# A state-space convolution with a gated token update: the second exponential table as raw products, sums finished in PSUM, and a written-out instruction order

## The chip, the core and the metric

The kernel runs on one core of one Trainium2 chip. A core has five instruction streams: PE (TensorE, matrix products into the accumulator memory PSUM), ACT (ScalarE, functions and scaled copies), DVE (VectorE, elementwise work), POOL (GpSimd) and SP (used here to issue transfers). They meet only at semaphores. The metric is device time in microseconds (us), the median of some runs.

## What is computed

A sequence of 2048 tokens with 512 channels goes through two branches and a sigmoid gate mixes them. Everything is bf16 in and out.

```python
g = sigmoid((x * gate_w).sum(-1, keepdims=True))     # x = A_u, [1, 2048, 512]
# branch a: long convolution by a diagonal state-space model, 128 states per channel
dt = exp(log_dt)[:, None];  A = A_re + 1j*A_im;  dB = dt*(B_re + 1j*B_im)
l = arange(2048).astype(bfloat16)                    # so large lags coincide
P = exp((dt*A)[:, :, None] * l[None, None, :])
K = einsum("dn,dnl,dn->dl", C, P, dB).real           # C = C_re + 1j*C_im
a = irfft(rfft(pad(x.T)) * rfft(pad(K)))[:, :2048].T + x * Dskip
# branch b: the 2 tokens with the largest x @ w_r get a feed-forward update
y = (silu(x_sel @ w_gate) * (x_sel @ w_up)) @ w_down * sigmoid(r_sel)
b = x + scatter_add(zeros, idx, y)
out = g * a + (1 - g) * b
```

## The kernel before

Channels are worked on in two halves of 256 (index h), tokens in two blocks of 1024 (blk). Transforms are matrix products with cosine and sine matrices; pm is the half of the frequencies, par the parity of a token, part the real or imaginary part. The stages, by the names in the code:

- **Parameters.** Six transposing transfers (`prm_t`) bring the 512 x 128 parameter matrices in with states on partitions. DVE makes the decay rate `AL`, the angle `B16` as a fraction of a turn, and the weights `WW`, C times dB.
- **Tables.** A lag is split as T1[s] + T2[j]: 32 coarse and 21 fine values. `exps1` and `exps2` take exponentials of both (ACT); `trig` scales the angles, takes sines, adds a quarter turn and takes sines again (ACT and DVE in turn); `tab1(h)` multiplies magnitude and sine into the first table TP, real and imaginary. `tab2(h)` makes 9 entries of the second table, multiplies them by `WW` (`cmul`, 9 entries wide) and gets the other 12 by two more complex products (8 and 4 wide): 26 DVE multiplies and adds per half. The magnitudes of half 1 are parked in DRAM and loaded back (`PK`).
- **Kernel values.** `kgen(h)` multiplies TP by the second table on PE, 64 groups of 4 channels, a real and an imaginary product of 84 columns (21 lags x 4 channels) each. Small products with rows of the identity (L765 to L771) keep the lags of the matching channel and bring lags to partitions: tile KC.
- **Spectra.** `kspec(h)` multiplies KC by seven operands KP of cosines and sines (`KUSE`), giving the kernel's spectrum KK for both blocks. `forward` gives the input's spectrum X: per block, group of frequencies, pm and part, eight products of 512 columns. For pm = 1 the odd tokens use a negated matrix NG, loaded again for each group. In block 1 one more product adds block 0's spectrum to it (L733, the carry).
- **Products.** `products(h, qd, blks)` multiplies spectra on DVE in pieces of 2048 and 1024 elements and leaves the result in X.
- **Router.** `routing` transposes the input on PE, gets the gate g and the router's scores, finds the two tokens, gathers them by products with one-hot columns and runs the feed-forward part. `xupd` adds the update to the input on PE (32 products of 512 columns) and ACT scales it by 1 - g, in place in U.
- **Output.** `inverse(h)` transforms X back in PSUM. ACT scales by g into YA and DVE adds it to U, or, for the last block of half 1, one DVE operation per 256 columns does both (L396). Sixteen transfers write the result.

The order of the work is not written by hand. Every operation is entered with what it reads and writes (`Prog.op`), a cost in us and a priority; `Prog.schedule` builds each engine's list by a simulation with these costs, choosing the operation that can start first, and where two engines can do an operation (`EV`, `SCL`, which copy or scale on ACT or DVE) the engine too. `Prog.emit` turns dependences into semaphore waits. The exponentials come first, then one load of ACT's function table, then the sines. Nearly all vector multiplies come from the helper `TT` (L389), copies out of PSUM from `EV` (L404), angle scalings from `SCL` (L408).

Of the kernel before, what the change touches and what calls it, by code (L numbers as in the profile page):

```python
# [58 lines left out]
class Prog:  # L59
# [119 lines left out]

    def emit(self, handles_sem, dsem):  # L180
# [53 lines left out]
    def run(self, e, h):  # L234
        last = None
        for o, waits in self.prog[e]:
            for k, v in waits:
                h.wait_ge(self.sems[k] if not isinstance(k, tuple) else self.dsem[k[1]], v)
            if o.tset is not None and o.tset % 2 != last:
                last = o.tset % 2  # L240
                if last:
                    h.preload_act_table_set("silu_and_others")
            r = o.fn(h)
            s, i = (self.dsem[o.sem], 16) if o.dma else (self.sems[e], 1)
            if isinstance(r, (list, tuple)):
                for x in r:
                    x.then_inc(s, i)
            else:
                r.then_inc(s, i)
        if e == SP:  # L250
            for o in self.finals:
                h.wait_ge(self.dsem[o.sem], 16 * o.n)
# [6 lines left out]
T2 = [0, 1, 2, 3, 258, 256, 512, 768, 4, 5, 6, 7, 262, 260, 516, 772, 1024, 1280, 1536, 1792, 2048]  # L259
T2BASE = [(0, 4), (13, 17), (8,)]  # L260
NJ = len(T2)
ANG2 = [124 + t for t in T2[:8]] + [1148, 1024, 4]
MAG2 = [None] + T2[1:8] + [1024, 4]
NM = len(MAG2)
KUSE = [(0, 0), (0, 1), (0, 2), (0, 3), (0, 4), (1, 4), (1, 5)]
# [13 lines left out]
def fwd_mats():  # L279
    th = theta(512)  # L280
    out = np.zeros((128, 2, 4, 2, 512))
    for par in range(2):
        for st in range(4):
            t = 256 * st + 2 * np.arange(128) + par
            out[:, par, st, 0] = np.cos(np.outer(t, th))
            out[:, par, st, 1] = -np.sin(np.outer(t, th))
    return out.reshape(128, -1)
# [12 lines left out]

def kspec_mats():
    lq = bf16_lag(np.arange(L))
# [6 lines left out]
    out = np.zeros((len(KUSE), 128, 2 * BLK))  # L309
    cover = np.zeros(L, dtype=bool)  # L310
    for q in sorted(set(lq.tolist())):
        j, s = where[q]
        for u, (i, jg) in enumerate(KUSE):
            if jg != j // 4:
                continue
            ls = np.nonzero(lq == q)[0]
            ls = ls[(ls >= BLK * i) & (ls < BLK * (i + 1))]
            cover[ls] = True
            t = ls - BLK * i
            out[u, 32 * (j % 4) + s, :BLK] = np.cos(np.outer(t, th)).sum(0)  # L320
            out[u, 32 * (j % 4) + s, BLK:] = (sg * np.sin(np.outer(t, th))).sum(0)
# [3 lines left out]

KB = 1024


def bass_gated_mix__ssm_conv_s4__moe_arch_mod__prompt_kernel(nc, A_u, A_A_re, A_A_im, A_B_re, A_B_im, A_C_re, A_C_im, A_log_dt, A_Dskip,
# [3 lines left out]
    eye = np.eye(128, dtype=np.float32)  # L333
    sgn = np.diag(np.where(np.arange(128) % 2 == 0, 1.0, -1.0))
    cb = np.concatenate([eye, np.zeros((128, 384), np.float32), sgn, -sgn], 1)
    cb_c = const(cb, "c_bf")
    cf = np.zeros((128, 160), np.float32)
    cf[:, 0:128] = eye
# [7 lines left out]
    cf[:, 147] = math.pi / 2  # L346
    cf_c = nc.inline_tensor(cf, "c_f32").ap()
    fm = fwd_mats()
    f_c = const(fm, "c_fwd")
    fn_c = const(-fm[:, 4096:], "c_fwdn")  # L350
# [3 lines left out]
    with ExitStack() as es:  # L354
# [8 lines left out]
        def B(name, off, nbytes, dt=BF):  # L363
            assert off + nbytes <= SBW and off % 2 == 0, (name, off, nbytes)
            return Buf(P, name, AR, "sb", int(off), int(nbytes), dt)
        class PB:
# [11 lines left out]
        def npe(n):  # L378
            return max(0.065, n * 0.00045)
# [33 lines left out]
        o_ = [190 * KB]  # L413
# [4 lines left out]
        CB = small("cb", 1536, BF); CF = small("cf", 640, F32); AL = small("al", 2048, F32); B16 = small("b16", 2048, F32)  # L418
        WW = small("ww", 2048, BF); SG = small("sg", 256, F32); SGB = small("sgb", 128, BF); RTS = small("rts", 1088, F32)
        OHT = small("oht", 64, BF); ZB = small("zb", 2048, BF); WL = small("wl", 16, BF); XS = small("xs", 16, BF)  # L420
        HB = small("hb", 448, BF); MSB = small("msb", 16, BF); DSK = small("dsk", 1024, BF); OHR = small("ohr", 4096, BF)
        assert o_[0] <= SBW, o_[0]
        oA, oB, oC, oD, oE, oF, oG, oI = [x * KB for x in (0, 16, 48, 64, 96, 117, 149, 170)]
        U = B("u", oA, 16 * KB)
        X = B("x", oB, 32 * KB)
        P.bufs.remove(X)
        XB = [[B("x%d%d" % (h_, k_), oB + (16 * h_ + 8 * k_) * KB, 8 * KB) for k_ in range(2)] for h_ in range(2)]
        xk = lambda h_, k_, *key: (XB[h_][k_], key)
        F = B("f", oC, 16 * KB)
        PRM = B("prm", oB, 6 * KB)  # L430
        LDT = B("ldt", oB + 6 * KB, 1 * KB); DTB = B("dtb", oB + 7 * KB, 1 * KB)
        TMP = [B("tmp%d" % i, oB + (8 + 2 * i) * KB, 2 * KB, F32) for i in range(4)]
        CM1 = B("cm1", oB + 16 * KB, 4 * KB, F32); CM2 = B("cm2", oB + 20 * KB, 4 * KB, F32); CMW = B("cmw", oB + 24 * KB, 4 * KB, F32)
        TP = [(B("tpi0", oD, 16 * KB), B("tpr0", oD + 16 * KB, 16 * KB)), (B("tpi1", oF, 16 * KB), B("tpr1", oF + 16 * KB, 16 * KB))]
        HQ = NJ * HC * 2
        TQ = [(B("tqi%d" % i, o, HQ), B("tqr%d" % i, o + HQ, HQ)) for i, o in enumerate((oE, oG))]
        XT = B("xt", oD, 16 * KB)
        WG = B("wg", oF, 14 * KB); WD = B("wd", oF, 14 * KB)
        WU = [B("wu%d" % i, oB + (8 + 16 * i) * KB, 7 * KB) for i in range(2)]
        EB = [B("eb%d" % i, o, NM * 512) for i, o in enumerate((oG, oE))]  # L440
        ST = B("st", oE, NM * 512)
        PK = Buf(P, "park", AR[:, :], "dram", 0, 4, BF)
        park = nc.dram_tensor("park", (128, NM * 256), BF).ap()
        QA = [B("qa%d" % i, o + NM * 512, 9 * KB) for i, o in enumerate((oG, oE))]
        BN = [(B("bni%d" % i, o + 14 * KB, KB), B("bnr%d" % i, o + 15 * KB, KB)) for i, o in enumerate((oG, oE))]
        NG = [B("ng%d" % i, oG + 16 * KB + 2 * i * KB, 2 * KB) for i in range(2)]
# [3 lines left out]
        KA = [B("ka0", oG, 64 * 84 * 2), B("ka1", oE, 64 * 84 * 2)]  # L450
        KC = [B("kc0", oD + 28 * KB, 3 * KB), B("kc1", oE + 11 * KB, 3 * KB)]
        KP = B("kp", oD, 28 * KB)
        KK = [B("kk0", oC, 16 * KB), B("kk1", oF, 16 * KB)]
        G = B("g", oF + 16 * KB, 16 * KB)
        PA = B("pa", oI, 4 * KB); PBb = B("pb", oI + 4 * KB, 4 * KB); PC = B("pc", oI + 8 * KB, 4 * KB); YY = B("yy", oI + 12 * KB, 4 * KB); YA = B("ya", oI + 16 * KB, 4 * KB)
# [4 lines left out]
        kgp = [PB("kg%d" % i, 2, i) for i in range(2)]  # L460
        mc = [0]
# [9 lines left out]
        def ngsrc(ft):  # L471
            return bass.AP(fn_c.tensor, fn_c.offset + ft * 128, [[4096, 128], [512, 8], [1, 128]])
# [9 lines left out]
        def prm_t(i):  # L482
            dp[0] -= 1e3
            P.op(SP, lambda h: h.dma_start_transpose(PRM(0, 128, i * D, (1, D)), dr(prm[i], 0, (128, D), (1, 128))), [], [(PRM, i)], cost=1.25, nbytes=131072, prio=dp[0])  # L484
        DQ([(LDT(0, 128, 0, (1, D)), dr(A_log_dt, 0, (0, 128), (1, D)))], [], [LDT], 131072, eng=ACT)
        DQ([(CB(0, 128, 0, (1, 768)), cb_c[:, :])], [], [CB], 196608, eng=ACT)
        P.op(ACT, ld_w, [], [WL], cost=1.0, n=2, nbytes=20000, dma=True, prio=2.5e5)
        prm_t(0)
        prm_t(1)
        for j in range(2):  # L490
            DQ([(U(0, 128, j * 8 * D, (2 * D, 4), (1, 2 * D)), dr(A_u, 1024 * j * D, (2 * D, 128), (256 * D, 4), (1, 2 * D)))], [], [(U, t) for t in range(8 * j, 8 * j + 8)], 1048576)
        for i in range(2, 6):
            prm_t(i)
        DQ([(F(0, 128, 0, (1, 8192)), f_c[:, :])], [], [F], 2097152)
        DQ([(CF(0, 128, 0, (1, 160)), cf_c[:, :])], [], [CF], 81920)
        for ft in range(2):
            DQ([(NG[ft](0, 128, 0, (128, 8), (1, 128)), ngsrc(ft))], [], [NG[ft]], 262144)
        DQ([(WG(0, 128, 0, (NF, 4), (1, NF)), dr(B_w_gate, 0, (NF, 128), (128 * NF, 4), (1, NF)))], [], [WG], 1835008)
        for buf, n in ((DSK, D), (OHR, L), (ZB, 2 * D)):
            P.op(POOL, lambda h, buf=buf, n=n: h.memset(buf(0, 128, 0, (1, n)), 0.0), [], [buf], cost=0.2 + n * 0.5e-3)  # L500
        DQ([(DSK(0, 1, 0, (1, D)), dr(A_Dskip, 0, (D, 1), (1, D)))], [], [DSK], 1024)

        IDN = lambda *a: CB(0, 128, *a)


        f512 = lambda b, c=0: b(0, 128, c, (1, D))
        AC(f512(DTB), f512(LDT), ACTF.Exp, [LDT], [DTB], tset=0)
        TT(f512(AL), f512(DTB), f512(PRM, 0), ALU.mult, [DTB, (PRM, 0)], [AL])
        TT(f512(TMP[0]), f512(DTB), f512(PRM, D), ALU.mult, [DTB, (PRM, 1)], [TMP[0]])
# [6 lines left out]
        def cbc(c):  # L516
            return PRM(0, 128, c, (0, 2), (1, D))
        TT(c2(CM1), c2(PRM, 2 * D), cbc(4 * D), ALU.mult, [(PRM, 2), (PRM, 3), (PRM, 4)], [CM1])
        TT(c2(CM2), c2(PRM, 2 * D), cbc(5 * D), ALU.mult, [(PRM, 2), (PRM, 3), (PRM, 5)], [CM2])
# [4 lines left out]
        for i in range(2):  # L524
            DQ([(WU[i](0, 128, 0, (NF, 2), (1, NF)), dr(B_w_up, 256 * NF * i, (NF, 128), (128 * NF, 2), (1, NF)))], [], [WU[i]], 917504)


# [9 lines left out]
        def exps2(ts):  # L537
            for b in (EB[0], ST):
# [415 lines left out]
```

## Time and profile before

The median of 3 runs is 193.42 us (193.13 to 194.49). The profiled execution has a span of 191.7 us.

| stretch of the span, us | PE busy | DVE busy | ACT busy | what runs |
|---|---|---|---|---|
| 0 to 40 | 24.93 | 24.23 | 33.39 | parameters, exponentials, router |
| 184 to 191.7 | 3.42 | 3.80 | 0.00 | last inverse, output |

The rows for the stretches in between, and the kernel's busiest groups, are read in the prediction. Of the groups not read there, these matter (group: line, engine, what, count, mean of one):

| group | count | mean ns |
|---|---|---|
| L731 PE, forward, 512 columns | 256 | 387 |
| L841 PE, inverse, 256 columns | 256 | 281 |
| L787 PE, spectra, 256 columns | 224 | 273 |
| L751 PE, table product, 84 columns | 256 | 200 |
| L404 ACT, copy of 1024 from f32 PSUM | 27 | 1021 |
| L404 DVE, the same | 5 | 1215 |
| L400 ACT, exponential of 512 | 41 | 619 |
| L400 ACT, sine of 1024 | 24 | 1052 |
| L408 ACT, angle scaling of 256 | 36 | 409 |
| L408 DVE, the same | 18 | 287 |
| L393 DVE, quarter turn added to 1024 | 12 | 681 |
| ACT, table load | 2 | 1283 |

A matmul's record is longer than the step from one to the next, since they are pipelined: the chain of waits shows the step. In the profile's lines, AR is the one SBUF buffer in which all tiles lie, and ps the PSUM.

### The profile page before, as it was taken

What the parts mean: (1) busy time and instruction counts of PE and PEld (TensorE: products, weight loads), DVE (VectorE), ACT (ScalarE), POOL (GpSimd) and SP (SyncE); (2) the same over time, 40 slices, a digit from 0 to 9 for tenths busy, and PEclk for the clock granted to TensorE, in tenths of its full rate; (3) what the DMA queues carried; (4) which work ended last, traced back from release to release, by engine and by line L of the source; (5) the groups of instructions that cost most, each with busy time, mean ns of one, the idle gap of its engine ahead of it and who ended that gap; (6) DMA issues with size and microseconds to landing.
All of it is one profiled execution on the core that took longest, in us unless ns stands there. A gap on an engine that the chain in (4) does not pass through costs nothing.

```text
span 191.7 us, 3562 instructions
## 1 busy us (share of the span) xinstructions
PE 160.6 (84%) x1490; PEld 105.7 (55%) x1490; DVE 163.5 (85%) x240; ACT 130.4 (68%) x214; POOL 3.9 (2%) x9
## 2 busy tenths in 40 slices
PE   0066499999999999999998798996899999659691
PEld 0065444666344444565563166785688888437580
DVE  0658745899999999996717999999999999999983
ACT  3679999999989995499959963697345562232400
POOL 8000000000000000000000000000000000000000
PEclk9999669999999999999999999999999999978999
DMA  5999999309401202200099200000920001012133
GB/s 94 257 289 359 294 404 405 100 9 329 104 14 45 55 4 51 55 3 0 15 364 419 108 2 3 0 3 0 359 84 0 3 0 55 3 55 65 45 109 109
DMA packets 22097, 22.39 MB, mean 117 GB/s; under 512 B 13121, under 2 KB 19394, under 8 KB 21698
## 3 DMA queue, kind: packets, MB, share of 16 engines
q1 hardware_dynamic: 20738, 21.84, 35.8%
q10 hardware_dynamic: 1344, 0.33, 1.5%
q8 instruction: 11, 0.18, 0.4%
q14 instruction: 4, 0.03, 0.0%
HBM read 18.63 MB, written 2.75 MB: 112 GB/s over the span
## 4 chain that ended last, share of the span: by engine, by line
PE 46%; DVE 40%; ACT 4%; DMA 4%; issue 2%; SPq 1%; DVEq 0%
DVE AR L389 38%; PE ps L731 30%; DMA AR<-in_A_u_dram 4%; PE ps L751 3%; PE ps L841 2%; ACT AR L400 2%; ACT AR L404 2%; PE ps L733 2%; PE ps L706 2%; DVE AR L396 2%; PE ps L765 2%; PE ps L620 1%; PE ps L695 1%; SPq L484 1%; PE ps L632 1%
## 5 line engine op out<-in xcount | busy, mean ns | idle before, releaser
L389 DVE TENSOR_TENSOR AR<-AR 128x1024 bf16<-128x1024 bf16 (+7 forms) x148 | 130.4, 939 | 11.4 <-DMA AR<-in_A_A_re_dram 6.2
L404 ACT ACTIVATE AR<-ps 128x1024 bf16<-128x1024 f32 (+5 forms) x58 | 45.2, 818 | 27.0 <-PE ps L787 14.5
L731 PE MATMUL ps<-AR 128*128 128x512 bf16 x256 | 60.5, 387 | 0.0
L400 ACT ACTIVATE AR<-AR 128x512 bf16<-128x512 f32 (+4 forms) x73 | 50.5, 757 | 3.4 <-DVE AR L389 2.2
L731 PEld LDWEIGHTS ps<-AR 128*128 128x128 bf16 x256 | 24.8, 99 | 28.9 <-issue 2.3
L841 PE MATMUL ps<-AR 128*128 128x256 bf16 x256 | 30.9, 281 | 6.0 <-DVE AR L389 4.4
L841 PEld LDWEIGHTS ps<-AR 128*128 128x128 bf16 x256 | 25.3, 101 | 11.1 <-DVE AR L389 5.8
L400 ACT ACTIVATE AR<-ps,AR 128x256 bf16<-128x256 f32 (+1 forms) x40 | 19.9, 566 | 15.6 <-PE ps L841 10.2
L787 PE MATMUL ps<-AR 128*128 128x256 bf16 x224 | 26.2, 273 | 2.5 <-ACT AR L404 2.5
L787 PEld LDWEIGHTS ps<-AR 128*128 128x128 bf16 x224 | 21.3, 98 | 7.2 <-ACT AR L404 4.6
L408 ACT ACTIVATE AR<-AR 128x256 int32<-128x256 f32 (+1 forms) x41 | 17.2, 488 | 0.0
L620 PE MATMUL ps<-AR 128*128 128x128 bf16 x64 | 6.7, 289 | 11.9 <-DMA AR<-in_A_u_dram 11.0
L393 DVE TENSOR_SCALAR AR<-AR 128x1024 int32<-128x1024 int32 (+5 forms) x22 | 11.5, 529 | 1.8 <-ACT AR L400 1.5
L620 PEld LDWEIGHTS ps<-AR 128*128 128x128 bf16 x64 | 5.7, 133 | 12.7 <-DMA AR<-in_A_u_dram 11.0
L751 PE MATMUL ps<-AR 128*128 128x84 bf16 x256 | 11.7, 200 | 1.1 <-ACT AR L404 1.1
L751 PEld LDWEIGHTS ps<-AR 128*128 128x128 bf16 x256 | 10.8, 97 | 3.1 <-ACT AR L404 1.5
L869 PE MATMUL ps<-AR 128*128 128x512 bf16 x16 | 6.2, 386 | 1.7 <-ACT AR L400 1.4
L404 DVE CAST AR<-ps 128x1024 bf16<-128x1024 f32 (+1 forms) x6 | 6.8, 1125 | 0.5 <-PE ps L733 0.5
L408 DVE TENSOR_SCALAR AR<-AR 128x256 int32<-128x256 f32 (+1 forms) x21 | 5.6, 306 | 1.6 <-ACT AR L400 1.5
L765 PE MATMUL ps<-AR 128*32 128x128 bf16 (+1 forms) x96 | 6.4, 383 | 0.5 <-ACT AR L404 0.5
L404 DVE COPY AR<-ps 128x1024 bf16<-128x1024 bf16 (+1 forms) x6 | 4.1, 688 | 3.0 <-PE ps L620 2.8
L733 PE MATMUL ps<-AR 128*128 128x512 bf16 x16 | 6.1, 379 | 0.0
(37 smaller groups left out, 57.6 us busy)
## 6 DMA issues: line engine op xcount, KB each, us to landing
AR<-c_ksp SPq DMA_DIRECT2D x1, 3584.0 KB, 14.4
AR<-in_A_u_dram SPq DMA_DIRECT2D x2, 1024.0 KB, 8.7
AR<-c_fwd SPq DMA_DIRECT2D x1, 2048.0 KB, 7.9
AR<-c_fwdn SPq DMA_DIRECT2D x8, 256.0 KB, 4.3
AR<-c_inv SPq DMA_DIRECT2D x1, 2048.0 KB, 9.0
out_dram<-AR SPq DMA_DIRECT2D x16, 128.0 KB, 2.2
AR<-in_B_w_gate_dram SPq DMA_DIRECT2D x1, 1792.0 KB, 11.2
AR<-in_B_w_up_dram SPq DMA_DIRECT2D x2, 896.0 KB, 11.7
```

The source lines that it names most:

```text
L389: return P.op(DVE, lambda h: h.tensor_tensor(out=o, in0=a, in1=b, op=op), rd, wr, cost=tt_cost(o, a, b), **k)
L393: return P.op(DVE, lambda h: h.tensor_scalar(out=o, in0=a, scalar1=s1, scalar2=None, op0=op0), rd, wr, cost=c, **k)
L400: return P.op(ACT, lambda h: h.activation(out=o, in_=a, func=func, scale=scale, bias=bias), rd, wr, cost=0.185 + nel(o) * 0.833e-3 + (0.09 ...
L404: return P.op((ACT, DVE), (lambda h: h.activation(out=o, in_=a, func=ACTF.Copy), lambda h: h.tensor_copy(o, a)), rd, wr, cost=(0.185 + n * ...
L408: return P.op((ACT, DVE), (lambda h: h.activation(out=o, in_=a, func=ACTF.Copy, scale=c), lambda h: h.tensor_scalar(out=o, in0=a, scalar1= ...
L620: last = h.transpose(bb(0, 128, db * 256 + t_ * 128, (1, 128)), U(0, 128, (2 * q + t_) * D + db * 128, (1, 128)), IDN(0, (1, 128)))
L731: last = h.matmul(o, w, U(0, 128, (blk * 8 + st * 2 + par) * D, (1, D)), start=(par + st == 0), stop=(par * 4 + st == 7 and blk == 0))
L733: last = h.matmul(o, CB(0, 128, 640 if part == 0 else 512, (1, 128)), X(0, 128, (1 - part) * 2048 + (pm * 4 + ft) * 256, (8192, 2), (1, 25 ...
L751: last = hh.matmul(pb(0, 128, (g - b0) * 84, (1, 84)), TP[h][1 - part](0, 128, g * 128, (1, 128)), TQ[h][1 - part](0, 128, g * 84, (1, 84) ...
L765: last = hh.matmul(pb(32 * g, 32, c4, (256, njg), (4, 64)), lw, KA[h](0, 128, c4 + 4 * (base[0] + g), (16, njg), (84, 64)), start=True, st ...
L787: last = hh.matmul(pb(0, 128, n * 256, (1, 256)), KP(0, 128, u * 2048 + tau * 128, (1, 128)), KC[h](0, 128, jg * 256, (1, 256)), start=(k ...
L841: last = hh.matmul(pb(0, 128, e * 256, (1, 256)), G(0, 128, ((par * 2 + part) * 4 + ft) * 512 + (2 * t2 + e) * 128, (1, 128)), X(0, 128, h ...
```

## The change

In seven parts. The lines below are the core of a diff of some 970 lines; "..." stands for what is left out.

**Order.** The scheduler's simulation is no longer called. `fixed` reads each engine's list from a string of operation numbers, and the engine of each two-engine operation from a string of digits. In that order a group of sines stands before the last 18 exponentials, with table loads around it, and the quarter-turn add may run on ACT.

```diff
+    def fixed(self, text, second):
+        seq = [int(text[3 * i:3 * i + 3], 36) for i in range(len(self.ops))]
+        order = {e: [] for e in ENGS}
+        for k, i in enumerate(seq):
+            o = self.ops[i]
+            if o.alt is not None:
+                e = list(o.alt)[int(second[i])]
+                o.eng = e
+                o.fn, o.cost = o.alt[e]
+            o.start = o.end = float(k)
+            order[o.eng].append(o)
+            o.pos = sum(1 for x in order[o.eng] if not x.dma)
+        self.order = order
...
             if o.tset is not None and o.tset % 2 != last:
+                if last is not None or o.tset % 2:
+                    h.preload_act_table_set(("exp_and_others", "silu_and_others")[o.tset % 2])
                 last = o.tset % 2
...
-        P.span = P.schedule()
+        P.fixed(ORDER, SECOND)
```

**Parameters.** Plain loads with 128 partitions of 4 rows, and 24 transposes on PE into PSUM, from which DVE's first products read.

```diff
+        def prm_l(i, **k):
+            DQ([(PRM(0, 128, i * D, (1, D)), dr(prm[i], 0, (512, 128), (1, 512)))], [], [(PRM, i)], 131072, **k)
...
+                for k in range(4):
+                    last = h.transpose(pps[q](0, 128, i * D + k * 128, (1, 128)), PRM(0, 128, (2 * q + i) * D + k * 128, (1, 128)), IDN(0, (1, 128)))
```

**Second table.** Four offset entries (`OFFS`) are multiplied by `WW`; the 17 others are an offset times a step (`STEP`). The complex product is left as four raw real products r[0] to r[3] (`RW`), and the sums over them are made by `kgen` in PSUM: four matmuls per group, of 84 and 68 columns, for two of 84. All halves' raw products lie in the same place, and the magnitudes of both halves stay in SBUF.

```diff
+STEP = [1, 2, 3, 258, 256, 512, 768]
+OFFS = [2048, 1024, 0, 4]
+RAWS = [(2, 0, 7), (3, 0, 7), (1, 4, 3)]
...
+        RW = [[B("r%d%d" % (i, h_), oR + RO[i], (NJ, NR)[i % 2] * 512) for i in range(4)] for h_ in range(2)]
+        DI = [B("di%d" % i, o, NM * 512) for i, o in enumerate((oTI[1] + 11 * NM * 512 // 11, oTI[0] + 21 * HC * 2))]
...
+            TS(nb(0, 128, 0, (4 * NOF, 64), (4, NOF), (1, 4)), w(2), -1.0, MUL, [(r[2], "w")], [nb])
+            for i, (a, b, ka) in enumerate(((eb, r[0], "w"), (di, nb, None), (eb, r[2], "w"), (di, r[0], "w"))):
+                o0 = NOF if i % 2 == 0 else 0
+                for k, (j, a0, n) in enumerate(RAWS):
+                    o = o0 + sum(x[2] for x in RAWS[:k])
+                    bw = 4 * NJ if b is not nb else 4 * NOF
+                    TT(r[i](0, 128, 4 * o, (4 * (NJ, NR)[i % 2], 64), (4, n), (1, 4)), a(0, 128, 4 * a0, (EW_, 64), (4, n), (1, 4)), b(0, 128, 4 * j, (bw, 64), (0, n), (1, 4)), MUL, ...
...
-                        for part in range(2):
-                            last = hh.matmul(pb(0, 128, (g - b0) * 84, (1, 84)), TP[h][1 - part](0, 128, g * 128, (1, 128)),
-                                             TQ[h][1 - part](0, 128, g * 84, (1, 84)), start=(part == 0), stop=(part == 1))
+                        for i in range(4):
+                            n, o = (W4, 0) if i % 2 == 0 else (4 * NR, 4 * NOF)
+                            last = hh.matmul(pb(0, 128, (g - b0) * W4 + o, (1, n)), TP[h][1 - i // 2](0, 128, g * 128, (1, 128)),
+                                             r[i](0, 128, g * n, (1, n)), start=(i == 0), stop=(i == 3))
```

**Forward.** The second half of the frequencies is the first half's sum minus twice the odd tokens. It is added in the same PSUM bank after the first half has been copied out: four matmuls for eight. NG holds the odd matrix times -2. The carry moves to the kernel's spectrum.

```diff
-                                for par in range(2):
+                                for par in range(pm, 2):
                                     for st in range(4):
...
-                                if blk:
-                                    last = h.matmul(o, CB(0, 128, 640 if part == 0 else 512, (1, 128)), ...
```

**Spectra.** Five operands for seven, in five buffers over the forward matrices, and the carry. Lags that round to 1024 or 2048 across a block's edge are taken out of them and handled as eight extra rows ("edge rows": `xed`, `sel3`, one DVE product of 256 per half).

```diff
-KUSE = [(0, 0), (0, 1), (0, 2), (0, 3), (0, 4), (1, 4), (1, 5)]
+KUSE = [(0, 0), (0, 1), (0, 2), (0, 3), (1, 4)]
...
+                                    last = hh.matmul(pb(0, 128, pm * 512, (1, 512)), CB(0, 128, 256 if part == 0 else 128, (1, 128)),
+                                                     KK[h](0, 128, (1 - part) * 2048 + pm * 1024 + 2 * qd * 256, (1, 512)), start=False, stop=True)
```

**Products.** The same operations; a product that went to a buffer of its own is put into the place of block 1's input instead.

**Output.** `xupd`, YA and the adds go. The diagonal matrix DG of (1 - g)/g, one DVE product of 2048, and one-hot rows OHR put the update and the input into the inverse's PSUM (`fin`), and one scaled copy by g per 256 columns, on ACT or DVE, finishes the output. OHR's rows are made after the second table product of half 1 (`late`), whose place they take.

```diff
+            TT(DG(0, 128, 0, (128, 16), (1, 128)), IDN(0, (0, 16), (1, 128)), SGB(0, 128, 64, (1, 16), (0, 128)), MUL, [CBI, (SGB, "x")], [DG])
...
+                                hh.matmul(pb(0, 128, e * 256, (1, 256)), DG(0, 128, tb[e] * 128, (1, 128)), U(0, 128, tb[e] * D + h * HC, (1, HC)), start=(e == 0), stop=False)
+                                last = hh.matmul(pb(0, 128, e * 256, (1, 256)), OHR(0, 128, tb[e] * 128, (1, 128)), ZB(0, 128, h * HC, (1, HC)), start=False, stop=False)
...
+                                P.op((ACT, DVE), (lambda hh, o=o, i_=i_, g_=g_: hh.activation(out=o, in_=i_, func=ACTF.Copy, scale=g_), lambda hh, o=o, i_=i_, g_=g_: hh.tensor_scalar(out=o, in0=i_, scalar1=g_, scalar2=None, op0=MUL)), ...
...
+        def late():
+            P.op(POOL, lambda h: h.memset(OHR(0, 128, 0, (1, L)), 0.0), [], [OHR], cost=1.2)
+            DMA([(OHR(32, NE, 0, (1, L)), oh_c[:, :])], [], [(OHR, "e")], NE * 4096)
```

## The prediction

> **What bounds the kernel now.** I read the page's slices first, to see which engine is full when.
>
> ```profile
> PE 160.6 (84%) x1490; PEld 105.7 (55%) x1490; DVE 163.5 (85%) x240; ACT 130.4 (68%) x214; POOL 3.9 (2%) x9
> ...
> PE   0066499999999999999998798996899999659691
> ...
> DVE  0658745899999999996717999999999999999983
> ACT  3679999999989995499959963697345562232400
> ```
>
> Each digit is 4.8 us. PE is full from about 24 to 103 us. DVE is full from 40 to 88 and again from 104 to 184, with a hole at 88 to 104. No engine is full throughout, so the shares alone decide nothing. The windows cut at those edges (columns: window, its length, then busy us and instructions of PE, PEld, DVE, ACT, POOL, clock, DMA share, GB/s) show the sizes:
>
> ```profile
> 40.00:88.00 48.00, 48.00 (x387) 24.53 (x386) 47.75 (x63) 41.87 (x70) 0.00 (x0) 1.00 0.25 67
> 88.00:104.00 16.00, 15.87 (x159) 8.95 (x157) 8.48 (x17) 13.21 (x22) 0.00 (x0) 1.00 0.53 203
> 104.00:184.00 80.00, 68.34 (x659) 53.30 (x660) 79.20 (x91) 41.98 (x70) 0.00 (x0) 0.98 0.17 57
> ```
>
> In the hole DVE lacks 16.00 - 8.48 = 7.5 us while PE works off the forward transforms. The timeline of the end gives the tail:
>
> ```profile
> 104.83 79.48 DVE L389 TENSOR_TENSOR AR<-AR 128x256 bf16<-128x256 bf16 x90 [0.35 <-ACT AR L400]
> ...
> 184.84 3.50 DVE L396 SCALAR_TENSOR_TENSOR AR<-ps,AR 128x256 bf16<-128x256 f32 x8 [0.54 <-PE ps L841]
> ```
>
> DVE multiplies without a break to 184.31; its first operation started at 6.23. Of 163.5 us busy, 3.5 lie in the tail, so 160.0 lie in those 178.1 us and 18.1 us are idle: 9.5 before 40 us, 7.5 in the hole, 1.1 elsewhere. The tail is 191.7 - 184.31 = 7.4. So the span is 6.2 + 160.0 + 18.1 + 7.4, and I forecast term by term. The median of the runs, 193.42, is 1.7 above this execution's span; I add 1.7 at the end.
>
> **Prices.** From the groups with shapes kept apart:
>
> ```profile
> L389 DVE TENSOR_TENSOR AR<-AR 128x2048 bf16<-128x2048 bf16 x60 | 70.7, 1216 | 0.3
> L389 DVE TENSOR_TENSOR AR<-AR 128x1024 bf16<-128x1024 bf16 x58 | 36.9, 682 | 4.3 <-PE ps L771 4.2
> L389 DVE TENSOR_TENSOR AR<-AR 128x2304 bf16<-128x2304 bf16 x12 | 15.9, 1350 | 0.1
> ```
>
> Adding the record lengths of the 90 operations above gives 85.0 us against 79.48 elapsed, so each costs its record less 0.06: 1.155, 0.62 and 1.29 us. Two rows give 0.52 ns per element plus 0.09 per operation; from that 1792 elements cost 1.02 and 768 cost 0.49.
>
> **Second table (DVE).** Per half, before: 6 x 1.29 + 6 x 1.155 + 10 x 0.62 + two of 512 (0.35) and two of 256 (0.22) = 22.0. After: 8 of 1792, 6 of 768, 10 of 1024 and one negation of 1024 (420 ns row, 0.36) = 8.2 + 2.9 + 6.2 + 0.4 = 17.7. Two halves: -8.7.
>
> **Output (DVE).** Six adds of 1024 go: -3.7 before the tail. Eight fused operations of the tail (479 ns) go; one scaled copy remains.
>
> **Moved between ACT and DVE by the fixed order.** DVE gains 13 angle scalings (287 ns, 0.23) and 4 negations (0.36), loses 4 quarter-turn adds of 1024 (0.62) and 2 of 768 (0.49), and has 13 PSUM copies for 11: +2.9 +1.4 -3.5 +1.0 = +1.8.
>
> **Added on DVE.** Six tiny operations of the routing (0.11 each), a PSUM copy of 512 (0.61), two multiplies of 256 from PSUM (no row; 0.22 to 0.42 by the bf16 row and the fused row, I take 0.42), and the diagonal matrix DG: 2048 outputs whose scalar repeats along the innermost dimension. No row shows that form: 1.155 if it runs like the 1216 ns row, 2.3 if like two copies of 1024 from f32 PSUM (1215 ns). I take 2.3, the bound that costs. Sum 0.7 + 0.6 + 0.8 + 2.3 = +4.4. [...] The parameter transposes only change where the first products read (f32 rate both ways, 0.69 per 512); one extra copy of 1024 is in the 13.
>
> DVE before the tail: 160.0 - 8.7 - 3.7 + 1.8 + 4.4 = 153.8.
>
> **PE.** Eight 512-column matmuls take 1.73 us in the chain, 0.216 each; 32 of the inverse take 3.67, 0.11 each; 24 of the table product take 0.90, 0.0375 each:
>
> ```profile
> 79.99 0.90 PE ps L751 x24
> 80.89 1.73 PE ps L731 x8
> ```
>
> Forward: 272 of 512 columns become 192, -17.3. The input update goes: -32 x 0.216 = -6.9. Spectra: 224 of 256 columns become 160, -7.0, plus 16 of 512 for the carry, +3.5. Table products: 256 more of 68 columns, from 256 x 0.03 to 256 x 0.0375, +9. Output terms: 64 of 256, +7.0. Transposes and edge rows: +4. Net -8. What counts is the place: forward, update and carry, -17.3 - 6.9, come out of the stretch that ended at 103, where the first half's table products add 4.5. So PE reaches those products about 15 to 20 us earlier, and the 7.5 us hole of DVE loses its cause.
>
> **ACT.** Sixteen update copies go (707 ns, -9.9), seven output copies come (471 ns, +2.7), one more exponential (+0.5), six adds (+5.3), seventeen scalings and negations go (-8.0), PSUM copies -1.3, and two more table loads. The trace has a load of 1283 ns, and the next operation starts 1.30 after it: +2.6. [...] Net about -8, and from 40 to 95 us ACT and DVE have some 50 us of work each, taking turns sine by sine: little slack there.
>
> **New waits.** (1) Both halves' second table lie in one place, and the second half's sine table lies over the first half's first table. So DVE's first write for half 1 waits for the last table product of half 0. Between the end of table 2 of half 0 and that write DVE has 14 us queued (8 first-table products 9.2, 3 adds, 3 negations, 7 scalings, a copy). The product is 256 matmuls, 8.8 us, but its evictions (596 ns, 10 of them on ACT) alternate there with 7 sines (1052 ns), 7 scalings and a copy of 1024: 5.0 + 6.7 + 2.2 + 1.0 = 15. Wait: 0 to 2, I take 2; without that cover it would be 9 to 15. (2) A forward bank's second sum waits for the copy of the first (1021 ns on ACT); the other bank's matmuls are queued between, so 0, at most 8 x 1.0 on PE. (3) Sync's queue: the one-hot load waits for a POOL memset (1811 ns) that waits for table product 1, and the 2 MB inverse matrix queues behind it (9.0 us to land). From about 117 that is 128; PE still has the selection and spectra of half 1 (13 us) then. Cost 0 to 2, hidden. (4) The five spectrum operands lie over the forward matrices, so their loads queue on SP behind the forward's last ones; four of them take 14.4 x 2048/3584 = 8 us by the row of the old load and are needed only when ACT has emptied the selection, some 10 us later: 0, at most 8. The parked exponentials' store and reload go; nothing on the path waited for them. (5) All eight transposed copies of the input sit on DVE, so the router's logits come some 4 us later and with them ACT's second batch of exponentials; ACT was late there before by as much, without two sine groups done.
>
> **Idle.** Start 6.3: plain loads (3.7 us for the log_dt row) plus eight transposes replace 5 us DMA transposes. Before 40 us: 9.5 becomes about 5.5, since sine groups now fill it. Hole: 7.5 becomes 2. Elsewhere 0.5. Sum 8. Tail: 7.0; two scaled copies on two engines close it instead of 0.9 us of DVE.
>
> 6.3 + 153.8 + 8 + 7.0 = 175.1, plus 1.7: **177**.
>
> **Rivals.**
> (A) as above, DVE bound, 177; alone 172 to 183. Chance 0.68.
> (B) The written order keeps DVE as idle as before, 18 instead of 8: 187. For it: an order fixed on modelled durations can't react, and ACT and DVE alternate. Against: 40 to 88 us had 0.25 us idle at nearly the same load. 0.14.
> (C) PE binds the last stage. From about 108 it has the products 8.8, selection 2.8, spectra 10.4, output terms 7.0, inverse 28: 57 us, ending at 165, under DVE's 168. At a granted clock of 0.8 (the window from 168 to 176 us has 0.79) 57 becomes 71: 179 + 4 + 1.7 = 185. 0.08.
> (D) Slower: weight loads bind the table product, since two matmuls now share what one did. PEld's record is 97 ns; if a matmul cost that, product 0 takes 24.8, DVE waits 10.7, and product 1 takes 24.8 in PE's last stage: 108 + 10.7 + 24.8 + 49 + 6 = 198. It passes 193 from about 88 ns. Against it: 24 matmuls with as many loads took 0.90. 0.05.
> (E) Hardly any idle left and DG fast: 170. 0.05.
>
> The range of 170 to 187 takes in A, and the near parts of B, C and E. About 1% either way can be told from no change. Faster by more: nearly all of A, B, C, E, 0.92. Within: 0.03. Slower: 0.05.
>
> **What would show it.** In the changed profile: DVE busy near 154 to 155 and idle under 12 after its start; the 1792 row near 1083 ns; the DG operation at 1.2 or 2.3; table products near 0.034 each; no hole in DVE between 88 and 104 but a wait of up to 2 for the table product; three table loads on ACT; a tail near 7. DVE idle of 15 or more means B, PE gapless from 105 on means C, table products above 0.08 mean D. I would be wrong in kind if ACT were the full engine from 40 to 95.

## The result, and the profile after

The changed kernel takes 172.76 us (171.93 to 172.91, 5 runs), 0.891 of the time before (95% interval 0.889 to 0.894). The forecast was 177 with a range of 170 to 187. The profiled execution has a span of 170.1 us.

The head of its page, busy times and slices (a digit is 4.25 us here):

```profile
PE 149.8 (88%) x1686; PEld 106.4 (63%) x1686; DVE 154.1 (91%) x248; ACT 123.8 (73%) x196; POOL 3.2 (2%) x8
...
PE   0607899989998999999988999999999999969980
...
DVE  0399999999999999999999999999999999999931
ACT  2499999999999999999995567755765434506152
...
PEclk9999999999999999999999999999999999999998
```

DVE has no hole left anywhere; ACT is as full as DVE until 88 us; PE never stands still for long after 20 us, and in this execution its granted clock doesn't fall before the end. The windows at the same edges as before (the columns are those of the prediction), with the last stage cut where it now ends:

```profile
0.00:40.00 40.00, 27.81 (x224) 17.19 (x225) 32.13 (x78) 34.20 (x56) 1.37 (x7) 1.00 0.84 300
40.00:88.00 48.00, 46.69 (x606) 27.53 (x604) 47.59 (x86) 47.88 (x75) 0.00 (x0) 1.00 0.19 67
88.00:104.00 16.00, 15.26 (x186) 11.64 (x185) 15.96 (x20) 9.83 (x14) 0.00 (x0) 1.00 0.12 35
104.00:162.00 58.00, 56.35 (x647) 47.01 (x643) 56.95 (x64) 28.79 (x48) 1.81 (x1) 1.00 0.19 63
```

DVE starts at 6.84 and ends its last product at 163.01 after 153.65 us of work. So the forecast's four terms read:

| term, us | before | forecast | after |
|---|---|---|---|
| start of DVE | 6.2 | 6.3 | 6.84 |
| DVE work | 160.0 | 153.8 | 153.65 |
| DVE idle | 18.1 | 8 | 2.52 |
| tail | 7.4 | 7.0 | 7.10 |
| span | 191.7 | 175.1 | 170.1 |
| median less span | 1.7 | 1.7 | 2.7 |

Of the 21.6 us that the span lost, 6.3 are work and 15.6 are idle time. The idle term is the one that was mis-sized, and most experiments ask what made it so small. DVE's idle time below is always counted like this, from its first operation to its last product, in the execution that was profiled.

The profiled execution, 171.93 us, was the fastest of the five; the four others have spans of 170.9 to 171.1 at a mean granted clock of 0.989 to 0.990 instead of 0.996, so in the median some 0.9 us, which no trace breaks down, come on top of these terms.

### The profile page after: what moved, and what is told of

Its sections match the earlier page's. It is cut to its first block, busy times and chain, and to the rows that moved or that the text cites. A ratio compares the mean times of both kernels' runs of the same rounds, so it can differ in the third digit from the quotient of the medians.

```text
span 170.1 us, 3961 instructions
## 1 busy us (share of the span) xinstructions
PE 149.8 (88%) x1686; PEld 106.4 (63%) x1686; DVE 154.1 (91%) x248; ACT 123.8 (73%) x196; POOL 3.2 (2%) x8
## 4 chain that ended last, share of the span: by engine, by line
DVE 44%; ACT 23%; PE 22%; issue 6%; DMA 2%; SPq 0%
DVE AR L479 38%; ACT AR L490 14%; PE ps L850 9%; ACT AR L494 5%; PE ps L915 5%; PE ps L867 3%; DVE AR L494 2%; DMA AR<-c_bf 2%; ACT L255 2%; DVE AR L498 2%; PE ps L984 2%; PE ps L815 2%; ACT AR L498 1%; DVE AR L668 1%; DVE AR L488 1%
## 5 line engine op out<-in xcount | busy, mean ns | idle before, releaser
L479 DVE TENSOR_TENSOR AR<-AR 128x2048 bf16<-128x2048 bf16 (+8 forms) x138 | 118.2, 902 | 1.2
L850 PE MATMUL ps<-AR 128*128 128x512 bf16 x192 | 44.3, 379 | 0.6 <-ACT AR L494 0.5
L984 PE MATMUL ps<-AR 128*128 128x256 bf16 x256 | 30.8, 273 | 2.0 <-DVE AR L479 1.9
L850 PEld LDWEIGHTS ps<-AR 128*128 128x128 bf16 x192 | 18.0, 99 | 22.2 <-issue 2.5
L984 PEld LDWEIGHTS ps<-AR 128*128 128x128 bf16 x256 | 24.8, 98 | 5.9 <-DVE AR L479 3.0
L992 ACT ACTIVATE AR<-ps,AR 128x256 bf16<-128x256 f32 x31 | 13.5, 473 | 18.5 <-PE ps L984 18.1
L915 PE MATMUL ps<-AR 128*128 128x256 bf16 x160 | 19.8, 273 | 0.7 <-ACT AR L494 0.7
L867 PEld LDWEIGHTS ps<-AR 128*128 128x128 bf16 x512 | 18.6, 98 | 1.3 <-ACT AR L494 0.3
L867 PE MATMUL ps<-AR 128*128 128x84 bf16 (+1 forms) x512 | 19.0, 198 | 0.1
L915 PEld LDWEIGHTS ps<-AR 128*128 128x128 bf16 x160 | 15.0, 98 | 5.3 <-ACT AR L494 2.3
L724 PE MATMUL ps<-AR 128*128 128x128 bf16 x64 | 7.7, 309 | 5.8 <-DVE AR L479 5.0
L498 DVE TENSOR_SCALAR AR<-AR 128x256 int32<-128x256 f32 (+1 forms) x38 | 11.0, 315 | 0.0
L724 PEld LDWEIGHTS ps<-AR 128*128 128x128 bf16 x64 | 6.3, 140 | 7.1 <-issue 6.3
L498 ACT ACTIVATE AR<-AR 128x256 int32<-128x256 f32 (+1 forms) x24 | 9.2, 438 | 0.0
L612 PE MATMUL ps<-AR 128*128 128x128 bf16 x24 | 2.9, 312 | 5.8 <-DMA AR<-c_bf 5.8
L971 PE MATMUL ps<-AR 128*128 128x256 bf16 x32 | 7.8, 273 | 0.1
L972 PE MATMUL ps<-AR 128*128 128x256 bf16 x32 | 7.7, 273 | 0.0
L494 DVE COPY AR<-ps 128x1024 bf16<-128x1024 bf16 x9 | 6.6, 743 | 0.4 <-PE ps L724 0.3
L612 PEld LDWEIGHTS ps<-AR 128*128 128x128 bf16 x24 | 2.4, 145 | 6.1 <-DMA AR<-c_bf 5.8
```

The lines of the kernel that those rows point to most:

```text
L479: return P.op(DVE, lambda h: h.tensor_tensor(out=o, in0=a, in1=b, op=op), rd, wr, cost=tt_cost(o, a, b), **k)
L494: return P.op((ACT, DVE), (lambda h: h.activation(out=o, in_=a, func=ACTF.Copy), lambda h: h.tensor_copy(o, a)), rd, wr, cost=(0.185 + n * ...
L498: return P.op((ACT, DVE), (lambda h: h.activation(out=o, in_=a, func=ACTF.Copy, scale=c), lambda h: h.tensor_scalar(out=o, in0=a, scalar1= ...
L724: last = h.transpose(bb(0, 128, db * 256 + t_ * 128, (1, 128)), U(0, 128, (2 * q + t_) * D + db * 128, (1, 128)), IDN(0, (1, 128)))
L850: last = h.matmul(o, w, U(0, 128, (blk * 8 + st * 2 + par) * D, (1, D)), start=(pm + par + st == 0), stop=(par == 1 and st == 3), skip_gro ...
L867: last = hh.matmul(pb(0, 128, (g - b0) * W4 + o, (1, n)), TP[h][1 - i // 2](0, 128, g * 128, (1, 128)), r[i](0, 128, g * n, (1, n)), start ...
```

## Experiments

Line numbers are those of each experiment's own code. Differences in us are against the 172.76 of the changed kernel, ratios against the kernel before as it was timed with that experiment (its median was 193.3 to 194.0), so differences below some 0.6 us say little.

**The order alone: e1_sched and e1b_engines.**

```diff
-        P.fixed(ORDER, SECOND)
+        P.schedule()
```

> The changed kernel's own operations, ordered by the list scheduler of the kernel before instead of by the written order; the scheduler also picks ACT or DVE for each copy and scaling, and puts all exponentials ahead of all sines (one table load after the first instead of three). Theory (the order is what took the idle time of DVE down to 2 us, against the 8 I had forecast): DVE idle between its first operation and its last product comes back to 8 to 12 us and the time is 178 to 184. Rival (the removed work alone did it, the order only writes down what the scheduler would do): DVE idle stays under 4 and the time is 172 to 175.

205.98 us, 1.060 of the kernel before (1.057 to 1.063). The same operations, in the scheduler's order, are slower than the kernel before. Slices of PE and its clock (5.1 us a digit), and two rows of PE's waits (us in total, times, longest):

```profile
PE   0559999469995039999991999999993873699991
...
PEclk9988999958589658999999699999999597999997
```

```profile
PE ps L850 <- ACT AR L494: 11.0, 1, 11.0
...
PE ps L915 <- DMA AR<-c_ksp: 4.5, 1, 4.5
```

Both are waits that the prediction listed as new and priced at nothing: the second forward sum behind the copy of the first on ACT (2), and the spectrum operands that lie over the forward matrices (4). DVE also waits 7.1 us at once for the second half's table product, a wait that the prediction didn't list. Behind PE's gaps the clock falls to 0.50, for 3.4 to 10.2 us at a time. DVE is idle for 29.1 us, far beyond the 8 to 12 that the theory gave, and the tail takes 14.7 instead of 7.1. Was it the order, or the scheduler's choice of engines?

```diff
+        for i, o in enumerate(P.ops):
+            if o.alt is not None:
+                o.eng = list(o.alt)[int(SECOND[i])]
...
+        P.schedule()
```

> The list scheduler again, but every copy, scaling and addition is pinned to the engine that the written order uses; only the order is the scheduler's. In e1_sched PE waited 11.0 us at once for a forward copy on ACT, 4.5 for the spectrum operands, and the granted clock read 0.5 after each of its long gaps; DVE was idle some 43 us. Theory (the order itself: forward copies and table evictions stand behind sines on ACT): the same gaps, 195 or more. Rival (the scheduler's choice of engines, 10 more copies and scalings on ACT, made ACT late): 175 to 185.

194.19 us, 0.999 of before (0.995 to 1.003): just under the theory's bound. With the written engines DVE is idle for 14.4 us, and the tail takes 14.7 here too, with 10.5 us of PE's work for the outputs left in it (both figures from an execution of 191.64 us). The same two waits, for a forward copy and for the second half's table product, are 4.8 and 4.9 at once. So with these operations the written order, its early sines among it, is worth 21 us against this scheduler's and the written choice of engines another 12. Without them the change gains nothing. The reverse, a written order for the operations of the kernel before, wasn't tried, so how much of the gain the order could have had alone isn't known.

**The raw products alone: e2_dvesum.**

```diff
+            for i in (0, 2):
+                s_ = r[i](0, 128, 4 * NOF, (4 * NJ, 64), (1, 4 * NR))
+                TT(s_, s_, r[i + 1](0, 128, 0, (4 * NR, 64), (1, 4 * NR)), ADD, ...)
...
-                        for i in range(4):
+                        for i in (0, 2):
```

> Only the raw products are undone: DVE adds the two raw halves of each table (4 additions of 4352 elements, 2.3 us each by 0.52 ns an element, +9.3 us on DVE) and TensorE multiplies them in 2 x 84 columns a block instead of 84+68+84+68 (256 matmuls of 68 fewer, about -8.5 us on PE). Theory (DVE is the bound throughout, as the sum of the forecast has it): 172.8 + 9.3 = 182, and the gain on PE buys nothing. Rival (PE or ACT sets the pace where the additions sit, so they partly fall into time that DVE would have lost): 173 to 177.

182.03 us (ratio to before 0.937, 0.935 to 0.939). DVE's work is 163.20, its idle time 3.8: of the 9.6 us more work 9.3 appear in the time, and PE's saving buys nothing. PE now waits for DVE in front of the table products:

```profile
PE ps L887 <- DVE AR L495: 8.2, 2, 4.2
```

Its granted clock also stood at 0.50 for 17 us of this run, which takes back a part of what it saved.

**The forward sums: e3_fwd and e3b_twice.**

```diff
-                                for par in range(pm, 2):
+                                for par in range(2):
...
-                                        last = h.matmul(..., start=(pm + par + st == 0), ...)
+                                        last = h.matmul(..., start=(par + st == 0), ...)
```

> Only the forward sums finished in PSUM are undone: each second sum is computed anew from 8 matmuls of 512 columns instead of 4 on top of the first, 64 more in all, 64 x 0.216 = +13.8 us on PE between about 20 and 100 us; nothing changes on DVE and ACT. Theory (PE has about 1.3 us to spare in 40 to 88 and 0.7 in 88 to 104, so it falls behind and DVE's hole before the products returns): +6 to +11, time 179 to 184, DVE idle 8 or more, most of it after 70 us. Rival (DVE's and ACT's queues cover it): within 2 us, 172 to 175.

194.02 us (1.001, 0.997 to 1.004): 21 us for 13.8 us of matmuls, more than either theory. DVE is idle for 25.0. One wait of PE sticks out, and the windows around it show what follows:

```profile
PE ps L915 <- DMA AR<-c_ksp: 8.4, 1, 8.4
```

```profile
102.50:104.00 1.50, 0.15 (x1) 0.00 (x0) 1.50 (x3) 0.00 (x0) 0.00 (x0) 1.00 0.24 35
104.00:105.50 1.50, 0.00 (x0) 0.00 (x0) 1.50 (x2) 0.00 (x0) 0.00 (x0) 1.00 0.91 268
105.50:107.00 1.50, 0.00 (x0) 0.00 (x0) 1.50 (x4) 0.00 (x0) 0.00 (x0) 0.73 0.99 401
107.00:111.00 4.00, 0.00 (x0) 0.00 (x0) 4.00 (x6) 0.00 (x0) 0.00 (x0) 0.50 0.94 386
111.00:114.50 3.50, 3.44 (x16) 2.27 (x16) 0.01 (x1) 0.00 (x0) 0.00 (x0) 0.50 0.01 6
...
116.00:117.50 1.50, 1.50 (x14) 1.25 (x13) 0.00 (x0) 0.89 (x2) 0.00 (x0) 0.86 0.00 0
```

PE's last matmul ends at 102.65. The clock (third column from the right) reads 1.00 until 105.5 and 0.73 in the next 1.5 us, so it fell to 0.50 at about 106.2 (worked out from the window's mean). PE works again from 111, still at 0.50, and 16 matmuls fill 3.44 us while DVE, in the fifth column, has nothing left to do. The clock is back at about 116.4. The edit makes the second sum read the forward matrices again, so they are held longer and the operands that lie over them load later. The next run adds the same work without that:

```diff
-                                for par in range(pm, 2):
-                                    for st in range(4):
+                                for par, st in [... for n in range(2 if pm == 0 and part == 0 else 1) ...]:
```

> The first sum of the first half of each forward bank is run twice, over itself, with the same result: again 64 matmuls of 512 columns more, 13.8 us on PE, in the places of e3_fwd, but each forward matrix is free as early as in the changed kernel. e3_fwd took 194.0, 21 us more, with 8.4 us of PE waiting for the spectrum operands (c_ksp, over the forward matrices) and a clock of 0.5 behind that gap. Theory (PE's own time is on the path from 25 to 105 us, so most of 13.8 is paid, and the 8.4 with the slow clock is the price of the matrices held longer): 183 to 188 and no wait for c_ksp over 2 us. Rival (it is PE's time alone that cost 21): 191 to 195.

185.89 us (0.961, 0.958 to 0.963), the clock at 1.00 in the mean and no wait for c_ksp among PE's largest. So PE's time is on the path: 13.1 us are paid of the 13.8 that 64 matmuls of 0.216 make, and DVE's idle time is 15.9. What the change took out of PE's forward sums is thus a second reason, beside the order, why DVE's holes are gone. The other 8 us of e3_fwd come with the matrices held longer, the wait for the load and the slow clock behind it; the two weren't tried apart.

**The early sines: e4_onetable.** In the written sequence, whatever hangs on a sine is moved behind the last exponential:

```diff
+        last0 = max(key[o.idx] for o in self.ops if o.tset == 0)
+        for o in sorted(self.ops, ...):
+            if key[o.idx] <= last0 and (o.tset == 1 or late_ & o.deps):
+                late_.add(o.idx)
```

> All exponentials before the first sine, so one table load instead of three after the first (-2.6 us on ACT); the four early sines and what hangs on them come some 9 us later, and what DVE and PE have otherwise in that stretch is moved ahead of them. Theory (the early sines are what filled DVE before 40 us, 1.0 us idle there where I forecast 5.5): DVE idle before 45 us rises by 5 or more and the time is 176 to 181. [...]

179.32 us (0.924, 0.921 to 0.926). Windows between 20 and 52 us of this run, and the first of them of the changed kernel:

```profile
20.00:28.00 8.00, 8.00 (x105) 5.24 (x104) 4.25 (x16) 8.00 (x16) 0.00 (x0) 1.00 1.03 406
...
36.00:44.00 8.00, 1.69 (x6) 0.53 (x5) 7.90 (x25) 3.88 (x7) 0.00 (x0) 0.68 0.42 148
44.00:48.00 4.00, 4.00 (x11) 1.24 (x10) 4.00 (x10) 3.27 (x6) 0.00 (x0) 0.50 0.01 4
48.00:52.00 4.00, 4.00 (x72) 2.50 (x71) 1.75 (x5) 3.70 (x6) 0.00 (x0) 0.86 0.00 0
```

```profile
20.00:28.00 8.00, 8.00 (x104) 5.26 (x102) 7.54 (x28) 7.88 (x11) 0.00 (x0) 1.00 1.03 405
```

DVE has 4.25 us of work between 20 and 28 instead of 7.54. PE has next to nothing from 36 to 44, its clock falls, and DVE pays for that too from 48 to 52. Idle time is 9.3 instead of 2.5. The two extra table loads cost 2.6 us on ACT, and the early sines are worth 6.6 us of the time after that is paid.

**One engine burdened: e7_act2 and e7_dve2.** Four sines, or four products, of half 1's first table run twice over themselves:

```diff
+            if twice:
+                AC(so(0), lo, ACTF.Sin, ks, [(s, "s")], scale=SC16, tset=ts)
```

> The four sines (not the cosines) of the first table of the second half are computed twice into the same place, +4.4 us on ACT between 55 and 80 us, nothing elsewhere. ACT is busy 47.9 of the 48 us from 40 to 88. Theory (ACT binds there together with DVE): +3 to +5, 176 to 178. Rival (only DVE binds, ACT is full because it is always given something): under +1, 172 to 173.8.

> The four sine products of the first table of the second half are computed twice into the same place, +4.8 us on DVE between 55 and 90 us, nothing elsewhere. Theory (DVE is the bound all along): +4.8, 177 to 178. Rival (ACT and PE set the pace in that stretch and DVE has some slack): +1 to +3, 174 to 176.

176.09 us (0.910, 0.908 to 0.911) and 177.26 us (0.916, 0.912 to 0.920): 3.3 and 4.5 us more. By the busy totals 4.0 us were added on ACT (127.8 for 123.8) and 4.6 on DVE's work (158.23 for 153.65), so 0.8 and nearly all of it is paid. By the intervals each share is known to some 0.2, so the two can't be told apart. The window from 40 to 88, with ACT burdened and then with DVE burdened:

```profile
40.00:88.00 48.00, 44.44 (x567) 26.15 (x575) 43.69 (x79) 47.84 (x74) 0.00 (x0) 0.96 0.17 59
```

```profile
40.00:88.00 48.00, 42.60 (x561) 25.64 (x570) 47.59 (x82) 43.86 (x70) 0.00 (x0) 1.00 0.19 68
```

The burdened engine stays full and the two others lose 2 to 4 us each: they wait for it. With ACT burdened DVE's quarter-turn adds wait 3.8 us for ACT instead of 0.3; with DVE burdened ACT waits some 6 us for DVE instead of 1.9.

**One engine relieved: e11_less.**

```diff
-                                    for st in range(4):
+                                    for st in range(2 * pm, 4):
```

> PE alone is relieved: half of each forward second sum (the matmuls of two of its four row blocks, 32 of 512 columns, 6.9 us between 25 and 95 us) is left out, so the odd spectra are incomplete; ACT and DVE have the same operations on other numbers. Adding 13.8 us there cost 13.1 (e3b_twice). Theory (ACT, DVE and PE are bound together up to 104 us, so one engine alone can't be relieved): -0 to -2, 170.8 to 172.8. Rival (PE holds the path and the others only follow it): -4 to -6.5, 166 to 169.

173.45 us (0.897, 0.893 to 0.901): no gain, though half of each second sum is left out; the theory had 0 to 2 us less. DVE keeps its 153.47 us of work, with 3.8 idle. Part of what PE saved it lost to its clock, which stood at 1.00 here in the profiled execution of the changed kernel:

```profile
20.00:24.00 4.00, 3.79 (x22) 2.29 (x23) 3.56 (x9) 3.97 (x5) 0.00 (x0) 0.57 1.03 411
...
52.00:56.00 4.00, 3.72 (x13) 1.30 (x14) 3.89 (x10) 3.97 (x8) 0.00 (x0) 0.70 0.07 22
```

**A fourth engine: e8_pool.**

```diff
+            if P.cnt in IDS:
+                return P.op(POOL, lambda h: h.tensor_scalar(out=o, in0=a, scalar1=c, scalar2=None, op0=ALU.mult), ...)
```

> 20 of the angle scalings between 40 and 88 us (11 on ACT, 9 on DVE) go to POOL, which does nothing there: about -3.6 us on ACT and -2.1 on DVE by their rows (411 and 291 ns, less the overlap of 0.08); PE unchanged. e7 had +4.4 on ACT cost 3.3, +4.8 on DVE 4.5, and e3b +13.8 on PE 13.1. Theory (the stretch is bound by ACT and DVE in turns): -1.5 to -2.5, 170.3 to 171.3. Rival 1 (PE is full there as well and holds the path alone once they are relieved): within 1 us. Rival 2 (POOL is slow, so sines wait for their angles): slower by 2 us or more, with ACT idle behind POOL in the profile.

179.22 us (0.927, 0.925 to 0.929): the second rival. From the groups by shape (busy us, mean ns, then idle time before them and its cause):

```profile
L515 POOL TENSOR_SCALAR AR<-AR 128x256 int32<-128x256 f32 x20 | 26.9, 1352 | 47.5 <-ACT AR L506 46.7
L506 ACT ACTIVATE AR<-AR 128x1024 bf16<-128x1024 int16 x24 | 24.6, 1050 | 4.4 <-POOL AR L515 4.3
```

A scaling takes 1352 ns on POOL in the mean, and the sines (L506 here) wait for it. DVE, with nine scalings fewer, still has 154.43 us of work, since some of its operations ran slower beside POOL (the last section), and 8.9 idle.

**DG on ACT: e5_dgact and e10_edge.**

```diff
-            TT(DG(0, 128, 0, (128, 16), (1, 128)), IDN(0, (0, 16), (1, 128)), SGB(0, 128, 64, (1, 16), (0, 128)), MUL, ...)
+            for tb, at in zip([*range(8, 16), *range(8)], (...)):
+                AC(DG(0, 128, tb * 128, (1, 128)), IDN(0, (1, 128)), ACTF.Copy, ..., scale=SG(0, 128, 96 + tb, (1, 1)))
```

> The diagonal matrix DG is built by 16 scaled copies of 128 columns on ACT (some 0.3 us each, put into gaps of ACT between 112 and 127 us, where it is busy about two thirds of the time) instead of one DVE operation whose record is about 2.5 us; the output terms read it block by block. -2.4 us on DVE, +4.8 on ACT, nothing on PE. Theory (DVE binds the last stage): -1.5 to -2.4, 170.4 to 171.3. Rival (PE binds there too, 56.4 us busy of the 58 from 104 to 162, or late evictions on ACT hold it up): within 1 us of the changed kernel, 172 to 174.

172.14 us (0.890, 0.888 to 0.892), not to be told from the changed kernel. DVE has 2.1 us less work, and one new wait, in front of the edge rows' product:

```profile
DVE AR L495 <- PE ps L917: 1.6, 1, 1.6
```

That product reads a selection which PE finishes at 118.4. Moved two operations down DVE's list:

```diff
+        key = {i: 481.5 if self.ops[i].orig == 465 else k for i, k in key.items()}
```

> e5_dgact again, with one small DVE product (8 x 256, the edge rows of half 1, which reads a late selection in PSUM) two operations later on DVE. In e5_dgact DVE waited 1.64 us there for PE, which ate most of the 2.1 us that DG's move had freed (172.1 against 172.8). Theory (that one wait is what ate it): -1.2 to -1.6 against e5_dgact, 170.5 to 171. Rival (PE itself is full from 104 to 162, 56.4 of 58, and now ends last): within 0.5 of e5_dgact, 171.6 to 172.2.

170.76 us (0.882, 0.879 to 0.885), against 0.891 (0.889 to 0.894) for the changed kernel: 2 us faster for 2.1 us of DVE's work, the best version here.

```profile
104.00:162.00 58.00, 57.48 (x677) 48.58 (x676) 56.76 (x64) 33.98 (x65) 1.81 (x1) 1.00 0.20 65
```

PE is now busy for 57.48 of the 58 us from 104 to 162, so I expect little more there from DVE alone; that wasn't tried.

## Why the prediction was right, and what was off

**Start, 6.3 forecast, 6.84 measured.** I counted the parameter loads. What came last was the identity for PE's transposes, third on SP's queue, landed at 5.72.

**DVE work, 153.8 and 153.65.** The multiplies of 1792 took 1080 ns where two rows gave 1083:

```profile
L479 DVE TENSOR_TENSOR AR<-AR 128x1792 bf16<-128x1792 bf16 x16 | 16.6, 1080 | 0.0
L479 DVE TENSOR_TENSOR AR<-AR 128x2048 bf16<-128x2048 bf16 x49 | 59.7, 1242 | 0.5
```

DG, taken at the slow bound of 2.3, took 2.28; it is one of the 49 operations of 2048, and without it e5_dgact has 48 with a mean of 1219 ns. e2_dvesum, the raw products undone, came out at the sum of DVE's terms. PE's and ACT's sums, -8 each, are -10.8 and -6.6 by the busy totals; the forecast added up neither.

**Idle, 8 and 2.5: the mis-sized term.** Its parts were 5.5 before 40 us (measured 1.0 after the start), 2 for the wait on the table product (0), and 0.5 elsewhere (1.5). For the first I let the early sines fill part of the old gap and counted the rest on; e4_onetable shows that they fill it, at 6.6 us of the time: without them 5.4 us are idle there, the figure that I had put down for having them. For the second I set PE's evictions against DVE's queue and took a wait from a range that began at 0; table product 0 ended at 82.4, and DVE has no wait above 0.33 us between its start and the tail. That the hole of 7.5 would lose its cause was right, though PE gained less on it than I said: its forward matmuls end 13 us earlier (89.6 for 102.8) and table product 0 12 (82.4 for 94.5), not 15 to 20.

**New waits at nothing.** In the changed kernel that held: PE's largest wait for a forward copy is 0.5 us, and after its start it waits for no transfer. But the waits are there when something moves: e1_sched waited 11.0 us for the one and 4.5 for the other, e3_fwd 8.4. The bound of 8 for the first was too low: it counted eight copies of 1 us, and the 11.0 are a single copy that stood behind ten us of other work in ACT's list. With the same operations these waits come and go with the order, so it is the written order that hides them.

**Rival B** gave the written order 14% to be no better than the list scheduler, since an order fixed beforehand can't react. The runs turn this about: it is the scheduler's order, made from the kernel's cost figures, that leaves DVE idle for 14 to 29 us with these operations.

**Rival C** (PE binds the last stage at a clock of 0.8) didn't come: PE had 56.35 us of work in 58, at a clock of 1.00. But the stage is nearly as full on PE as on DVE, so the sign that I named for C, PE without gaps from 105 on, all but came and doesn't tell C from A. What does is e10_edge, where 2.1 us less on DVE gained 2. **Rival D** is refuted by the table product, 256 matmuls in one row:

```profile
101.20 9.20 PE L867 MATMUL ps<-AR 128*128 128x84 bf16 x256
```

That is 0.036 us each, 84 and 68 columns in turn and each with a weight load of 98 ns beside it; 88 ns would have been needed. **Rival E** comes nearest: hardly any idle time, but without the fast DG.

**The bound.** I called it DVE. That predicts the sum, but it isn't the whole: from 40 to 88 us ACT is as full, and PE nearly so up to 104. At the places tried 1 us more cost 0.8 on ACT, 1.0 on DVE and 0.95 on PE (e7_act2, e7_dve2, e3b_twice), and 6.9 less on PE gained nothing. So the condition that I named for being wrong in kind, ACT full from 40 to 95, is half met (to 88), with DVE full beside it.

The median lies 2.7 above the profiled span, where I had added the 1.7 of before: 1.8 lie between this execution's time and its span, and the other 0.9 between it and the median. That the total is off by only 4 where the idle term alone was 5.5 too high is luck: the start was 0.5 too low and this step 1.0.

## What to carry to other kernels

Where several engines are full in one stretch, a sum over one of them still gives the time, but only an order that keeps all of them fed makes it true: price an edit's new waits with the order they will meet, and keep their bounds in mind when either changes. To learn what binds, run an operation twice over itself on each engine in turn and see how much of it is paid; where several are full, that taking work from one gains nothing doesn't say which of the others binds. And a free engine helps only after its own price is measured.

## What the runs showed of the hardware

In two runs a gap of PE cost more than its own length, since the clock stayed low behind it. In e3_fwd the granted clock fell to 0.50 some 3.5 us after the last matmul, and stayed there for 5.4 us after PE had work again; in e4_onetable it was still at 0.50 from 44 to 48 with PE busy throughout, and came back 6.0 us after PE's work had set in again at 43.1. Each stretch at 0.50 that ends within the span, in these two and in the other runs, lasts 3.41 us or a whole multiple of it (6.83 and 3.41 in the kernel before). Counted back in steps of 3.41 us, both returns come at the end of the first step that began with PE at work (113.0 to 116.4, 45.7 to 49.1). What sets these steps no run shows.

But the 3.41 us ahead of a fall weren't always idle by PE's record: in e4_onetable PE worked for 0.9 us of them. In e3_fwd the clock is also at 0.50 from 51.57 to 54.98 (0.93 in the mean of the window from 40 to 64), where PE had no gap; shortly before, it ran 112 matmuls of two columns each:

```profile
48.02 2.94 PE L803 MATMUL ps<-AR 128*128 128x2 bf16 x112
```

In e2_dvesum, e5_dgact, e7_act2 and e10_edge one such fall follows the same 112. In the profiles of the changed kernel, e3b_twice, e4_onetable, e7_dve2 and e8_pool they ran without one. Whether these matmuls have to do with the falls no run here tests.

In e8_pool POOL needed 1352 ns in the mean (844 to 4435) for a scaling of 256 f32 to int32 that takes 291 on DVE and 411 on ACT in the changed kernel. Beside it some of DVE's operations took longer: the six scalings of that shape that ran while POOL was at one took 423 ns in the mean, the fifteen others 295; for the quarter-turn additions it is 821 (three) and 690 (five).

A table load on ACT is 1283 ns, and the next operation starts 1.29 us after the load's start, at each of the three switches of the changed kernel, with 0.1 us of idle time ahead of the three together:

```profile
L255 ACT ACT_TABLE_LOAD x3 | 3.8, 1283 | 0.1
```

All exponentials ahead of the sines, with two loads fewer, cost 6.6 us in e4_onetable, since DVE and PE wait for the sines too.
